# Loading the accumulators of the second half later, behind small VectorE fills, in a one-core kernel of a gated long convolution and a two-layer ReLU network

## The chip, the core and the metric

The kernel runs on one core of a Trainium2 chip. The core has five engines that run side by side and wait for one another through semaphores: TensorE (PE in the profile; PEld is its weight load), VectorE (DVE), ScalarE (ACT), GpSimd (POOL) and SyncE (SP). SP does no arithmetic here; it issues most of the DMA transfers, one after another, in a fixed order. The metric is the device time of one execution in microseconds (us). Before the change the median of three runs is 1064.95 us (1064.24 to 1065.45).

## The reference, cut to what matters

`x` is `A_q`, 2048 rows of 576 columns, in float32. With `xn = layernorm(x)` the output is

```python
k_shift = short causal convolution of k (4 taps per channel)
kv = k_shift * v
y  = long causal convolution of kv with ssm_k per channel   # by FFT, length 2 * 2048
A  = xn * (y + kv * ssm_D)
h  = relu(xn @ w1)               # 576 -> 4608
B  = h @ w2                      # 4608 -> 576
out = x + A + B
```

## The kernel before

**The network.** The 2048 rows are 16 row tiles t of 128 rows (T = 16), in four blocks of four (BT = 4): block 0 is t 0 to 3, block 1 is 4 to 7, block 2 is 8 to 11, block 3 is 12 to 15. The 4608 hidden columns are 18 pairs of 128 (NPAIR = 18). The first half of the program takes blocks 0 and 1 through all pairs, the second half blocks 2 and 3. Its outer loop walks over `visits`, numbered q: each visit is one pair n of hidden columns (n from 18 on in the second half) for one block in place s (0 or 1). A visit of the second half has four stages, st 0 to 3 (`quad`): a Strassen-like set of products into two PSUM banks (tiles `psa` and `psb`, line 542) with a few VectorE additions (lines 597 and 600) between them, then the ReLU, split into a rounded high part `hh` (ACT, line 548) and the remainder `ll` (DVE, line 549). All matrices are split in such high and low parts, so that three float32r products make up one float32 product.

**The sums.** After each stage `fill()` takes up to two units from a queue of work. A unit (line 629) multiplies `hh` and `ll` by `w2` for one row tile and one half of the 576 columns, into one of three PSUM tiles `pso`, and DVE adds it to the accumulator `acc` (line 634 or 638). The accumulators hold x at first: `load_acc(t)` loads the rows of tiles t and t + 1 into one SBUF tile, in two DMAs of 288 KB (helper `load_x`, DMA line 160). There are only eight rows' worth of places, two pair tiles for each of two tags. Blocks 0 and 3 share one tag, blocks 1 and 2 the other. So the place of the pair (12, 13) is free only when the finished sums of the pair (0, 1) have been stored to `fin` (line 646, DMA of 576 KB), 14 follows 2, 8 follows 4 and 10 follows 6. In the names below `acc12` is the pair tile (12, 13), and `fin<-acc0` is the store of the pair (0, 1).

**The convolution.** It runs as a second stream of instructions (`conv()`), of which `tick()` places a piece between the matmuls of the network whenever the network's cost has grown enough. Its part `fm` is just beginning where the change lies: for each group g it loads two tiles of 288 KB, `ztk` and `ztx` (line 886; `ztk2` is that of k in group 2), splits each on ACT into `hik` or `hix` (line 893) and on DVE into `lok` or `lox` (line 894), multiplies by a 128 x 128 matrix into PSUM tiles `psf` (line 904, three places), copies the results for k out on ACT (lines 934 and 935), moves half of each by a DMA inside SBUF (`k<-k`, lines 937 and 938), copies those for x out swapped (`sw`, lines 945 and 946) and multiplies the two on DVE (line 947).

**The weights.** For each coming pair SP loads `both_w1` (lines 440 and 442) and `r2` (line 449); ACT rounds them (lines 466 and 528), POOL makes the low parts (line 428) and, in the second half, the sums of blocks of w1 (line 495).

**What sets the order.** The order on each engine is written into the program before it runs. It comes from a scheduler that places each instruction when a model of the machine says it is ready, in the order of the program; `here()` ties an instruction behind the latest accumulation and the latest ACT instruction of the network, so that it isn't placed early. SP then issues in that fixed order and stops at the first DMA whose semaphores aren't there. SP's DMAs also take eight landing counters in turn (DMAHW0 to DMAHW7 in the listings below), and each waits until the DMA that last used its counter, eight places ahead, has landed.

In the kernel before, all four loads are called behind the last stage of a visit:

```python
        if half == 1 and m == 0:
            base = HT + (1 - second) * BT
            for t in range(base, base + BT, 2):
                load_acc(t)
```

Of the kernel before, what the change touches and what calls it, by code (L numbers as in the profile page):

```python
# [22 lines left out]
T = S // P  # L23
# [5 lines left out]
NPAIR = DFF // FC  # L29
HR = 256  # L30
NB = 4
BT = T // NB
HALVES = 2
HB = NB // HALVES
HT = T // HALVES
# [74 lines left out]
def h3_ffn_kernel(ctx: ExitStack, tc, x, k, v, shift_k, ssm_k, ssm_D, w1, w2, fwd, inv, mid, out):  # L110
    nc = tc.nc
# [37 lines left out]
    def place(b):  # L149

        return 1 - b if b < HB else b - HB

    def halves(u):

        return slice(u * A1, (u + 1) * A1), slice((1 - u) * A1, (2 - u) * A1)

    def move(tile_, rows, t, store=False, queues=(nc.sync, nc.sync)):
        for u in range(U):
            a, b = tile_[halves(u)[0]], rows[u, :, t]
            queues[u].dma_start(*((b, a) if store else (a, b)))  # L160

    pairs = {}

    def load_x(t, tag, bufs, **queues):
        pair = xp.tile([P, 2, D], F32, tag=tag, name=f"acc{t}", bufs=bufs)
        move(pair, x, slice(t, t + 2), **queues)
        return pair

    def load_acc(t, **queues):
        pairs[t] = load_x(t, f"acc{place(t // BT)}", BT // 2, **queues)  # L170
        acc[t], acc[t + 1] = pairs[t][:, 0, :], pairs[t][:, 1, :]

    def stats(t, src):
        st = xp.tile([P, 2, 6], F32, tag="bn", name=f"bn{t}", bufs=4)
        for h in range(2):
            nc.vector.bn_stats(st[:, h, :], src[:, h * NH:(h + 1) * NH])  # L176
        nc.vector.bn_aggr(mv[:, t, :], st)

    def inv_std(t0, n):

        q = xp.tile([P, 3, BT], F32, tag="q", name=f"q{t0}")[:, :, :n]
        va, h0, qu = q[:, 0, :], q[:, 1, :], q[:, 2, :]
        nc.vector.tensor_scalar(va, mv[:, t0:t0 + n, 1], EPS, None, op0=OP.add)
        nc.scalar.activation(h0, va, AF.Sqrt, scale=0.25)
        nc.vector.reciprocal(qu, h0)
        nc.vector.tensor_tensor(qu, va, qu, OP.mult)
        nc.vector.scalar_tensor_tensor(qu, qu, 0.25, h0, op0=OP.mult, op1=OP.add)
        nc.vector.reciprocal(rstd[:, t0:t0 + n], qu)

    def normalized(dst, src, t, cols=slice(0, D)):  # L190
        nc.vector.tensor_scalar(dst[:, cols], src[:, cols], mv[:, t, 0:1], rstd[:, t:t + 1],
                                op0=OP.subtract, op1=OP.mult)
# [21 lines left out]
    def split_low(c, ps, s):  # L214

        if c == 4:
            xr = ops[s, "xr"]
            done["act"] = nc.scalar.activation(xr[:64, :], ps[:64, :], AF.Copy)
            done["dve"] = nc.vector.tensor_tensor(xr[64:, :], ps[:64, :], xr[:64, :],
                                                  OP.subtract)  # L220
            return None
        to = ops[s, "b2" if c % 2 else "b1"][:, :, c // 2]
        last = nc.scalar.activation(to[:, 0], ps, AF.Copy)  # L223
        nc.vector.tensor_tensor(to[:, 1], ps, to[:, 0], OP.subtract)  # L224
        return last

    def row_tiles(s, name):
        t = scratch(s, name)
        return [t[:, i * D:(i + 1) * D] for i in range(BT)]

    def plain_tiles(s):
        for name in ("b1", "b2", "xr"):
            operand(s, name)
# [37 lines left out]
    def turned(c, xn):  # L271
        w = min(P, D - c * P)
        ps = fft_psum()
        for i in range(BT):
            nc.tensor.transpose(ps[:w, i * P:(i + 1) * P], xn[i][:, c * P:c * P + w], ident)
        return ps

    def second_stats(srcs):
        for t in range(BT, BT + 2):
            with tc.issue_after(lows[0].ins):  # L280
                stats(t, srcs[t])

    def second_xT(srcs):

        s = place(1)
        plain_tiles(s)
        with tc.issue_after(done["acc"].ins):
            for t in range(BT + 2, HT):
                stats(t, srcs[t])
            inv_std(BT, BT)  # L290
        xn = row_tiles(s, "xn1")
        for cols in (slice(0, P), slice(P, D)):
            for i, row in enumerate(xn):
                normalized(row, srcs[BT + i], BT + i, cols)
        yield
        for cs in ((0, 1, 2), (3, 4)):
            for c in cs:
                split_low(c, turned(c, xn), s)
            yield
# [146 lines left out]
    def load_w2(n, h):  # L446
        f0 = (n % NPAIR) * FC
        r2 = wp.tile([P, FT, NH], F32, tag="r2", name=f"r2_{n}_{h}", bufs=2)
        nc.sync.dma_start(r2, w2[f0:f0 + FC, h * NH:(h + 1) * NH]
                          .rearrange("(j p) d -> p j d", p=P))  # L450
        raw_w[n, h] = r2
# [72 lines left out]
    def split_w2(n, h):  # L524
        r2 = raw_w[n, h]
        t = wp.tile([P, 2, FT, NH], F32R, tag="w2", name=f"w2_{n}_{h}", bufs=4)
        with at_turn(n):
            nc.scalar.activation(t[:, 0], r2, AF.Copy)  # L528
        last = split_lo(t[:, 1], r2, t[:, 0])
        weights[n]["w2", h] = t  # L530
        return last
# [25 lines left out]
    def mm1(n, s, j):  # L557
        g = weights[n][j]
        ps = bank(j, f"psh{n}_{s}_{j}")
        seq = []  # L560
        for c in range(4):
            b = ops[s, "b2" if c % 2 else "b1"][:, :, c // 2]
            seq += [(g[:, 0, c], b[:, 0]), (g[:, 0, c], b[:, 1]), (g[:, 1, c], b[:, 0])]
        seq += rest(n, j, s)
        for i, (a, m) in enumerate(seq):
            done["pe"] = nc.tensor.matmul(ps, a, m, start=i == 0, stop=i == len(seq) - 1)  # L566
            if i % 7 == 6:
                tick(W_PLAIN / 4)
        relu(n, s, j, ps)
# [88 lines left out]
    def fill():  # L658
        room = 2
        while work and work[0][0] <= room:  # L660
            size, args = work.pop(0)
            unit(*args)
            room -= size
# [23 lines left out]
    @contextmanager  # L687
    def here():


        with tc.issue_after(done["acc"].ins), tc.issue_after(done["act"].ins):
            yield
# [433 lines left out]
    visits = [(0, place(0)), (1, place(0)), (0, place(1)), (1, place(1))]  # L1126
# [36 lines left out]
    def later_w2(n, h):  # L1163
        with tc.issue_after(done["act"].ins):
            split_w2(n, h)
        if n + 1 < HALVES * NPAIR:
            load_w2(n + 1, h)
# [3 lines left out]
               (3, 0): [(split_plain, 2, 0)], (3, 1): [(split_plain, 2, 1)],  # L1171
               (3, 3): [(split_rest, 2), (load_w1, 4)],
               (5, 1): [(later_w2, 2, 0)], (6, 0): [(later_w2, 2, 1)]}
    rest_of_block = second_xT(acc)
    for q, (n, s) in enumerate(visits):
        half, m = divmod(n, NPAIR)
        b = HB + s if half else 1 - s
        second = q % 2
        if q == 2:
            for _ in rest_of_block:  # L1180
                fill()
        parts = quad(n, s, q % 2) if half else None
        for st in range(4):
            if half:
                next(parts)
            elif st % 2 == 0:
                mm1(n, s, st // 2)
                if q < 2:
                    done["acc"] = lows[-1]
            if q == 0 and st == 2:  # L1190
                second_stats(acc)
            for what, *args in opening.get((q, st), ()):
                what(*args)
            if q > 3:
                split_next(n, second, st)
                if st == 1 and n > 2:
                    later_w2(n, second)
            if half:
                tick(W_STAGE[st])
            if q > 3 and (st % 2 or st == 2 and q % 2):  # L1200
                next(ahead, None)
            fill()
        if m == NPAIR - 1 and not half:
            fetch(s, ("b1", "b2", "xr"))
        if n == NPAIR - 2 and not half:
            for _ in ahead:
                pass
            fetch(s, ("t",))
        last = m == NPAIR - 1
        if q in (1, 3):  # L1210
            phase([0, 1], s, b, False)
        elif q > 3 and second == 0:
            phase([n] if m == (0 if half else 2) else [n - 1, n], s, b, last)
        elif last:
            phase([n], s, b, True)
        if half == 1 and m == 0:
            base = HT + (1 - second) * BT
            for t in range(base, base + BT, 2):
                load_acc(t)
    while work:  # L1220
        fill()
    rest_of_stream()
# [27 lines left out]
```

## Time and profile before

| | |
|---|---|
| median of 3 runs | 1064.95 us (1064.24 to 1065.45) |
| the profiled execution's own time | 1063.99 us |
| its span (first to last instruction) | 1062.2 us |
| time of the execution that lies outside the span | 1.8 us |
| mean granted TensorE clock | 0.998 of full speed |
| engine busy shares: PE, DVE, ACT, POOL | 99%, 70%, 52%, 38% |
| moved by DMA | 204.45 MB, mean 192 GB/s |

The profile names instructions by the line of the kernel and by tiles without their numbers: `acc<-in_x` is any load of line 160 into an accumulator. A row of the timeline gives the start and the duration in us, the engine, line, operation, and in brackets how long the engine was idle just before and what ended that. SPq is the queue of DMA issues on SP: the duration of such a row is that of the issue, not of the transfer. Of several merged issues (x2) the duration covers any wait between them.

### The profile page before, as it was taken

The numbers are of one execution on the slowest core, as the hardware profiler recorded it, in microseconds if no ns is written. First come the engines' busy times: TensorE is split into PE (matmuls) and PEld (weight loads), VectorE is DVE, ScalarE is ACT, GpSimd is POOL, SyncE is SP. The second block draws the span as 40 slices with busy tenths as digits, with TensorE's granted clock in tenths as the row PEclk, the third lists the DMA queues.
The fourth block names the chain that finished last, engine by engine and source line by source line (L and its number), as shares of the span: only waits on it lengthen the run. The fifth ranks groups of instructions, "written<-read, shape, count | busy, mean of one in ns | idle before, by whom it ended". The sixth has DMA issues, their size and how long they took to land.

```text
span 1062.2 us, 20038 instructions
## 1 busy us (share of the span) xinstructions
PE 1048.8 (99%) x7153; PEld 989.5 (93%) x7153; DVE 744.0 (70%) x1312; ACT 551.3 (52%) x1201; POOL 398.6 (38%) x398
## 2 busy tenths in 40 slices
PE   8999999999999999999989999999999999999998
PEld 5889999989999999999989999999999999999997
DVE  4539778787777788772458787878777873666664
ACT  4226566534343443433267877687777773443441
POOL 4133333333332233243324434334333444544641
PEclk9999999999999999999999999999999999999999
DMA  9944867687566766856876656666566648776964
GB/s 225 208 97 133 226 173 209 203 229 205 152 192 175 205 193 181 262 144 216 255 197 185 176 171 180 175 192 189 163 178 190 182 126 255 225 224 215 287 193 112
DMA packets 156303, 204.45 MB, mean 192 GB/s; under 512 B 32845, under 2 KB 122703, under 8 KB 155180
## 3 DMA queue, kind: packets, MB, share of 16 engines
q1 hardware_dynamic: 143308, 189.00, 60.8%
q0 software_dynamic: 12576, 13.44, 5.6%
q8 instruction: 56, 0.92, 0.4%
q10 hardware_dynamic: 320, 0.74, 0.3%
q14 instruction: 43, 0.35, 0.1%
HBM read 133.92 MB, written 55.05 MB: 178 GB/s over the span
## 4 chain that ended last, share of the span: by engine, by line
PE 93%; DMA 3%; DVE 2%; ACT 1%; issue 1%; SPq 0%; DVEq 0%; ACTq 0%
PE pso L629 41%; PE psh L566 22%; PE psb L542 12%; PE psf L904 7%; PE psa L542 6%; PE psf L684 3%; DMA acc<-in_x 1%; DMA fin<-acc 1%; PE psf L1048 1%; PE psf L1050 1%; DMA ztk<-zk 1%; DMA zy<-vo 0%; ACT hh L548 0%; DVE bn L176 0%; DVE k L965 0%
## 5 line engine op out<-in xcount | busy, mean ns | idle before, releaser
L629 PE MATMUL pso<-w,hh 128*128 128x288 f32 x2304 | 469.5, 295 | 1.6 <-ACT w L528 0.8
L629 PEld LDWEIGHTS pso<-w,hh 128*128 128x128 f32 x2304 | 373.1, 188 | 9.9 <-ACT w L528 1.2
L629 PE MATMUL pso<-w,ll 128*128 128x288 f32 x1152 | 329.8, 295 | 0.0
L428 POOL TENSOR_TENSOR g<-both_w,g 128x256 fp32r<-128x256 f32 (+2 forms) x145 | 168.2, 1167 | 373.6 <-ACT g L466 320.3
L566 PE MATMUL psh<-b,g 128*128 128x512 f32 x864 | 218.2, 395 | 0.5 <-ACT b L223 0.2
L629 PEld LDWEIGHTS pso<-w,ll 128*128 128x128 f32 x1152 | 213.5, 188 | 1.1
L566 PEld LDWEIGHTS psh<-b,g 128*128 128x128 f32 x864 | 156.9, 188 | 30.5 <-DVE b L224 0.5
L638 DVE TENSOR_TENSOR acc<-pso,acc 128x288 f32<-128x288 f32 x232 | 101.8, 450 | 60.3 <-PE pso L629 59.1
L428 POOL TENSOR_TENSOR w<-r,w 128x576 fp32r<-128x576 f32 x72 | 113.4, 1576 | 56.1 <-ACT w L528 56.0
L548 ACT ACTIVATE hh<-psh 128x512 fp32r<-128x512 f32 x72 | 43.0, 598 | 144.2 <-PE psh L566 144.2
L549 DVE SCALAR_TENSOR_TENSOR ll<-psh,hh 128x512 fp32r<-128x512 f32 x72 | 49.4, 687 | 69.8 <-ACT hh L548 69.4
L542 PE MATMUL psb<-t,g 128*128 128x256 f32 x648 | 94.9, 280 | 0.1
L542 PEld LDWEIGHTS psb<-t,g 128*128 128x128 f32 x648 | 85.5, 188 | 0.4 <-DVE psa L597 0.3
L466 ACT ACTIVATE g<-both_w 128x256 fp32r<-128x256 f32 (+2 forms) x145 | 76.3, 543 | 9.5 <-PE psb L542 6.4
L495 POOL TENSOR_TENSOR both_w<-both_w 128x256 f32<-128x256 f32 x72 | 62.6, 890 | 33.7 <-DMA both_w<-in_w 32.4
L542 PE MATMUL psa<-b,g 128*128 128x256 f32 x432 | 63.1, 280 | 0.0
L548 ACT ACTIVATE hh<-psa 128x512 fp32r<-128x512 f32 x36 | 21.5, 597 | 72.3 <-PE psa L542 72.1
L542 PE MATMUL psb<-b,g 128*128 128x256 f32 x432 | 57.5, 281 | 0.0
L542 PEld LDWEIGHTS psa<-b,g 128*128 128x128 f32 x432 | 56.6, 188 | 0.0
L542 PEld LDWEIGHTS psb<-b,g 128*128 128x128 f32 x432 | 54.4, 188 | 0.2
L947 DVE TENSOR_TENSOR k<-psf,k 128x288 f32<-128x288 f32 x64 | 28.9, 453 | 35.5 <-ACT sw L946 34.2
L670 POOL DMA_DIRECT2D wx<-in_fwd x32 | 17.7, 552 | 95.4 <-PE psf L684 86.7
(134 smaller groups left out, 1697.6 us busy)
## 6 DMA issues: line engine op xcount, KB each, us to landing
r<-in_w SPq DMA_DIRECT2D x72, 288.0 KB, 4.4
zy<-vo SPq DMA_DIRECT2D x64, 288.0 KB, 3.1
zo<-zy SPq DMA_DIRECT2D x32, 576.0 KB, 4.5
both_w<-in_w SPq DMA_DIRECT2D x35, 512.0 KB, 4.2
zk<-zk SPq DMA_DIRECT2D x64, 144.0 KB, 2.5
ztk<-zk SPq DMA_DIRECT2D x32, 288.0 KB, 3.0
ztx<-zx SPq DMA_DIRECT2D x32, 288.0 KB, 3.6
k<-k SPq DMA_DIRECT2D x64, 144.0 KB, 3.4
```

The lines of the kernel that those rows point to most:

```text
L428: return nc.gpsimd.tensor_tensor(dst, src, hi, OP.subtract)
L466: nc.scalar.activation(hi, src, AF.Copy)
L495: nc.gpsimd.tensor_tensor(dst, a, b, op)
L542: done["pe"] = nc.tensor.matmul(ps, a, m, start=start and i == 0, stop=i == len(seq) - 1, skip_group_check=not start)
L548: done["act"] = nc.scalar.activation(hh, ps, AF.Relu)
L549: lows.append(nc.vector.scalar_tensor_tensor(ll, ps, 0.0, hh, op0=OP.max, op1=OP.subtract))
L566: done["pe"] = nc.tensor.matmul(ps, a, m, start=i == 0, stop=i == len(seq) - 1)
L629: done["pe"] = nc.tensor.matmul(ps[:, :NH], a, m, start=c == 0, stop=c == len(seq) - 1)
L638: done["acc"] = nc.vector.tensor_tensor(acc[t][:, dc], ps[:, :NH], acc[t][:, dc], OP.add)
L684: nc.tensor.matmul(ps[:, :NH], w[:, n, :], stk, start=n == 0, stop=n == 1)
L904: nc.tensor.matmul(ps[:, :NH], a, m[:, cols], start=n == 0, stop=n == 2)
L947: nc.vector.tensor_tensor(k1[:, cols], ps, k1[:, cols], OP.mult)
```

## The change

`load_x` may first write a zero into one column of each of the two rows of the pair (a DVE MEMSET of 128 x 2 elements), held by `here()`, and the two DMAs then wait for that fill. The four loads are called from a table, ahead of the units of the named stage: the pair 12 in stage 1 and the pair 14 in stage 2 of visit first_q + 1 (pair n = 18, place 0), the pair 8 in stage 2 and the pair 10 in stage 3 of visit first_q + 2 (n = 19, place 0). The call behind the last stage is gone. first_q is the visit of n = 18 in place 1.

```diff
-    def load_x(t, tag, bufs, **queues):
+    def load_x(t, tag, bufs, late=False, **queues):
         pair = xp.tile([P, 2, D], F32, tag=tag, name=f"acc{t}", bufs=bufs)
+        if late:
+            with here():
+                nc.vector.memset(pair[:, :, :1], 0.0)
         move(pair, x, slice(t, t + 2), **queues)
         return pair
...
+    first_q = visits.index((NPAIR, place(T // BT - 1)))
+    acc_loads = {(first_q + 1, 1): [T - BT], (first_q + 1, 2): [T - BT + 2],
+                 (first_q + 2, 2): [HT], (first_q + 2, 3): [HT + 2]}
...
                 if st == 1 and n > 2:
                     later_w2(n, second)
+            for t in acc_loads.get((q, st), ()):
+                load_acc(t, late=True)
             if half:
                 tick(W_STAGE[st])
...
-        if half == 1 and m == 0:
-            base = HT + (1 - second) * BT
-            for t in range(base, base + BT, 2):
-                load_acc(t)
```

In the listings below a row is the line, the operation and its tiles; lines of the changed kernel are higher by 3 from `load_x` on (line 886 is 889, 638 is 641). The first two listings are SP's queue from the store of the pair (2, 3) on. In the brackets stand the landing counters and engines that a DMA waits for. Before:

```order
L646 DMA fin_89<-acc2_100 128x1152 [waits DMAHW1_49,DVE_49]
L160 DMA acc14_5825<-in_x 64x1152 [waits DMAHW1_49]
L160 DMA acc14_5825<-in_x 64x1152
L646 DMA fin_89<-acc4_229 128x1152 [waits DMAHW4_49,DVE_49]
L886 DMA ztx1_5970<-zx_85 128x576 [waits DMAHW5_49,DVE_49]
L449 DMA r2_19_1_5883<-in_w2 128x2x288 [waits DMAHW6_49,Pool_49]
L160 DMA acc8_6019<-in_x 64x1152 [waits DMAHW7_49,DMAHW4_49]
L646 DMA fin_89<-acc6_232 128x1152 [waits DMAHW0_49,DVE_49]
L160 DMA acc8_6019<-in_x 64x1152
L160 DMA acc10_6022<-in_x 64x1152 [waits DMAHW2_49,DMAHW0_49]
L160 DMA acc10_6022<-in_x 64x1152 [waits DMAHW3_49]
L886 DMA ztk2_6007<-zk_86 128x576 [waits DVE_49]
```

The same stretch of SP's queue after the change:

```order
L649 DMA fin_89<-acc2_100 128x1152 [waits DMAHW7_49,DVE_49]
L160 DMA acc12_5879<-in_x 64x1152 [waits DMAHW2_49,DVE_49]
L160 DMA acc12_5879<-in_x 64x1152 [waits DMAHW1_49]
L160 DMA acc14_5927<-in_x 64x1152 [waits DMAHW7_49,DVE_49]
L160 DMA acc14_5927<-in_x 64x1152
L649 DMA fin_89<-acc4_229 128x1152 [waits DMAHW4_49,DVE_49]
L889 DMA ztx1_5972<-zx_85 128x576 [waits DMAHW5_49,DVE_49]
L452 DMA r2_19_1_5877<-in_w2 128x2x288 [waits DMAHW6_49,Pool_49]
L649 DMA fin_89<-acc6_232 128x1152 [waits DVE_49]
L889 DMA ztk2_6009<-zk_86 128x576 [waits DMAHW0_49,DVE_49]
L443 DMA both_w1_94<-in_w1 128x4x256 [waits DMAHW1_49,Pool_49]
L445 DMA both_w1_94<-in_w1 64x256 [waits DMAHW2_49,Pool_49]
```

The loads of 12 moved behind the store of (2, 3) (before they stood ahead of it); those of 14 stay behind that store, which they wait for through the counter DMAHW7; those of 8 and 10 no longer stand between the store of (6, 7) and `ztk2`. They now stand ten places further on, behind the load of `r2` of pair 20:

```order
L940 DMA k1_1_6011<-k1_1_6011 64x576 [waits Activation_49]
L941 DMA k2_1_6012<-k2_1_6012 64x576 [waits DMAHW1_49,Activation_49]
L452 DMA r2_20_0_6094<-in_w2 128x2x288 [waits DMAHW2_49,Pool_49]
L160 DMA acc8_6146<-in_x 64x1152 [waits DMAHW3_49]
L160 DMA acc8_6146<-in_x 64x1152 [waits DMAHW4_49]
L160 DMA acc10_6200<-in_x 64x1152 [waits DMAHW5_49]
L160 DMA acc10_6200<-in_x 64x1152 [waits DMAHW6_49]
L889 DMA ztk4_6216<-zk_86 128x576 [waits DMAHW7_49,DVE_49]
```

Their DVE wait is gone from these rows because an earlier DMA of the queue already waits for a later DVE instruction than the fills.

On DVE the first two fills stand between the accumulations of block 1 (`pso17_4_0` is pair 17, row tile 4, column half 0). After the change:

```order
L641 TENSOR_TENSOR acc4_229<-pso17_5_0_5850,acc4_229 128x288
L168 MEMSET acc12_5879 128x2
L552 SCALAR_TENSOR_TENSOR ll18_1_1_5803<-psb18_1_5678,hh18_1_1_5802 128x512
L641 TENSOR_TENSOR acc6_232<-pso17_6_0_5889,acc6_232 128x288
L641 TENSOR_TENSOR acc6_232<-pso17_7_0_5897,acc6_232 128x288
L168 MEMSET acc14_5927 128x2
L641 TENSOR_TENSOR acc4_229<-pso17_4_1_5935,acc4_229 128x288
L641 TENSOR_TENSOR acc4_229<-pso17_5_1_5943,acc4_229 128x288
L897 TENSOR_TENSOR lok0_5884<-ztk0_5776,hik0_5883 128x576
L600 TENSOR_TENSOR psa18_0_5823<-psb18_0_5822,m5_18_0_5836 128x256
```

Without the two MEMSET rows this is the order before. The fill of 12 waits for the landing of the store of (0, 1), the fill of 14 for that of (2, 3). The fills of 8 and 10 stand later on DVE, the first behind the addition of `pso18_15_0`, the second behind that of `pso18_13_1` and ahead of `lok2`.

The order of PE is the same in both kernels. On ACT two instructions change places, `w2_19_0` (line 528) and `hik2` (line 893). Before, and then after the change:

```order
L593 ACTIVATE psa19_0_6026<-psb19_0_6025 128x256
L528 ACTIVATE w2_19_0_6095<-r2_19_0_5727 128x576
L893 ACTIVATE hik2_6074<-ztk2_6007 128x576
L934 ACTIVATE k1_1_6009<-psf_6011 64x288
```

```order
L596 ACTIVATE psa19_0_6022<-psb19_0_6021 128x256
L896 ACTIVATE hik2_6070<-ztk2_6009 128x576
L531 ACTIVATE w2_19_0_6091<-r2_19_0_5727 128x576
L937 ACTIVATE k1_1_6011<-psf_6013 64x288
```

`hik2` now stands directly behind the copy into `psa`. On POOL two of the four sums of line 495 for pair 20 move ahead of the low part of `w2_19_0`.

## The prediction

> **What bounds the kernel now.** I read the busy shares first, then what PE waited for, then the chain of waits around the one long wait, and there the timelines of PE, ACT, SP and DVE. The shares, from the page, and PE's longest waits (us in total, times, longest):
>
> ```profile
> PE 1048.8 (99%) x7153; PEld 989.5 (93%) x7153; DVE 744.0 (70%) x1312; ACT 551.3 (52%) x1201; POOL 398.6 (38%) x398
> ...
> PE psf L904 <- ACT k L935: 4.0, 1, 4.0
> PE psw L1109 <- DVE table L1103: 1.2, 1, 1.2
> ...
> PE pso L629 <- ACT w L528: 0.8, 1, 0.8
> ```
>
> PE is the bound. All its waits but the first row belong to the start of the program. So time can be won in the middle only at that one place, a wait of 4.0 us of a convolution matmul for ACT. The chain of waits through it (start, length, what):
>
> ```profile
> 516.47 7.96 DMA fin<-acc
> ...
> 531.21 4.66 DMA fin<-acc
> ...
> 537.06 5.35 DMA ztk<-zk
> ...
> 543.48 0.41 ACT k L935
> ...
> 543.94 1.09 PE psf L904 x3
> ```
>
> Read backwards: PE waits for a PSUM place that ACT empties at line 935; ACT stood at `hik2`, which waits for the load `ztk2`; that load was issued only at 537.06. The timelines say why (PE, then ACT, then SP, and from the waits of SP the row for line 160):
>
> ```profile
> 539.62 0.30 PE L629 MATMUL pso<-w,ll 128*128 128x288 f32 x1
> 543.94 0.61 PE L904 MATMUL psf<-hix,m_sb 128*128 128x288 f32 x1 [4.02 <-ACT k L935]
> ...
> 535.81 0.67 ACT L528 ACTIVATE w<-r 128x576 fp32r<-128x576 f32 x1
> 542.49 0.68 ACT L893 ACTIVATE hik<-ztk 128x576 fp32r<-128x576 f32 x1 [6.01 <-DMA ztk<-zk]
> ...
> 516.47 0.37 SPq L646 DMA_DIRECT2D fin<-acc  x1
> ...
> 531.21 0.54 SPq L646 DMA_DIRECT2D fin<-acc  x1
> 531.79 5.21 SPq L160 DMA_DIRECT2D acc<-in_x  x3
> 537.06 0.58 SPq L886 DMA_DIRECT2D ztk<-zk  x1
> ...
> SPq L160 <- DMA fin<-acc: 16.0, 4, 7.6
> ```
>
> SP stands four times, 16.0 us together, at loads of x whose place a store still holds. The last time, behind 531.79, it stands at the loads of 10 until the store of (6, 7) has landed, near 535.9, and `ztk2` is behind them. This is the head-of-queue wait that the change takes away.
>
> The stall costs more than its 4 us:
>
> ```profile
> 500.56 3.19 PE pso L629 x24
> ...
> 20.00:22.60 2.60, 1.81 (x10) 1.24 (x9) 1.92 (x7) 2.05 (x4) 0.94 (x2) 1.00 1.11 321
> ...
> 543.94:546.96 3.02, 3.02 (x12) 3.02 (x13) 1.87 (x5) 2.92 (x7) 1.78 (x2) 0.51 1.04 246
> ```
>
> Elsewhere such a matmul follows the last after 3.19 / 24 = 0.133 us. Behind the stall (windows; the number behind the brackets is the granted clock) 12 matmuls took 3.02 us at a clock of 0.51. The short stall of 0.8 us at 21 us, inside the first window, left the clock at 1.00.
>
> **The change, part by part.**
>
> *Gone: the stall.* The matmul of 543.94 was due 0.133 us behind 539.62, at 539.75: 4.19 us. The slow clock: 3.02 - 12 x 0.133 = 1.42 us. Together 5.61 us, if nothing else stops PE there.
>
> The Trainium skill, page "TensorE: Matmul & The Clock Gate", section "Part 1: The HAM clock gate", says that an idle stretch of about 3.4 us halves the array's clock and that about as long a busy one restores it. The trace agrees: 4.02 us idle, then 0.51 for 3.02 us. By that rule a leftover stall under 3.4 us would lose no clock, so a stall half removed would still give back the 1.42 us.
>
> *Is `ztk2` early enough?* Without the loads ahead of it SP reaches it behind the store of (6, 7). Then it waits for its buffer, which `lox0` on DVE frees, and its landing counter for the loads of 12, issued over 10 us before. The DVE row, and two windows for the rate of the DMAs (the last number is GB/s):
>
> ```profile
> 530.40 1.13 DVE L894 TENSOR_TENSOR lox<-ztx,hix 128x576 fp32r<-128x576 f32 x1
> ...
> 513.50:524.50 11.00, 11.00 (x86) 10.82 (x86) 5.82 (x11) 3.81 (x8) 3.24 (x3) 1.00 0.77 213
> 524.50:535.90 11.40, 11.40 (x89) 11.23 (x88) 7.81 (x15) 6.03 (x15) 4.01 (x4) 1.00 0.82 259
> ```
>
> So `ztk2` goes out near 531.6 rather than 537.06. With the 5.35 us that it took before, it lands at 537.0. That is the late end, since the 1.18 MB of the loads of 8 and 10 no longer go out beside it. At 259 GB/s half of that is 2.3 us, which gives 534.7 as the early end. ACT comes to `hik2` at 535.8 either way (the row of `w2_19_0`, whose place it takes). I take 535.8.
>
> *The work that hides it from there.* What follows on ACT and DVE was packed tightly behind `hik2` in the trace. Its last two DVE rows, and the PE product behind them:
>
> ```profile
> 545.48 1.04 DVE L894 TENSOR_TENSOR lox<-ztx,hix 128x576 fp32r<-128x576 f32 x1 [1.15 <-ACT hix L893]
> 546.45 0.44 DVE L947 TENSOR_TENSOR k<-psf,k 128x288 f32<-128x288 f32 x1
> ...
> 548.16 0.87 PE L542 MATMUL psb<-t,g 128*128 128x256 f32 x6
> ```
>
> From the start of `hik2` to the end of the multiplication of line 947 it took 546.89 - 542.49 = 4.40 us. Now `w2_19_0` (0.67) lies in between: 535.8 + 4.40 + 0.67 = 540.9. PE needs that multiplication 18 matmuls after the old stall, at 539.75 + 18 x 0.133 = 542.1, for a PSUM place; the product of 548.16, which also needs the line 597 addition queued behind it on DVE, 21 matmuls after, at 542.5. So 1.2 us are to spare, and `ztk2` may land at 537.0 without stopping PE: the cost is nothing, covered by these 18 matmuls; each us beyond 537.0 costs one.
>
> *What is late next: the copies `k<-k`.* The multiplication also needs the copies of group 0, which stand behind the loads of `both_w1`, and those wait for POOL's low parts of g. The POOL row, SP's rows, and from the page the size and median landing time of such a copy:
>
> ```profile
> 532.83 1.44 POOL L428 TENSOR_TENSOR g<-both_w,g 128x256 fp32r<-128x256 f32 x2 [1.92 <-ACT g L466]
> ...
> 537.73 0.39 SPq L440 DMA_DIRECT2D both_w<-in_w  x1
> 538.22 1.11 SPq L442 DMA_DIRECT2D both_w<-in_w  x2
> 539.38 0.59 SPq L937 DMA_DIRECT2D k<-k  x1
> 540.07 0.54 SPq L938 DMA_DIRECT2D k<-k  x1
> ...
> k<-k SPq DMA_DIRECT2D x64, 144.0 KB, 3.4
> ...
> 545.18 4.04 POOL L495 TENSOR_TENSOR both_w<-both_w 128x256 f32<-128x256 f32 x4 [7.19 <-DMA both_w<-in_w]
> ```
>
> POOL is done at 534.3; SP then needs the same 2.34 us up to the second copy, 536.6. With 3.4 us it lands at 540.0, in time for 540.5, when by the same sum `lox1` (ended 546.52) leaves DVE. The other end is the crowded queue: `both_w1`, issued from 537.73, had landed only at 545.18. The last of its three issues began near 538.8, so took some 6.4 us; a copy so slow lands at 543.0, and the multiplication would end at 543.5, 1.4 us behind 542.1. Range 0 to 1.4 us; the row of the copies is the nearer, I take 0.3.
>
> *Added: four fills on DVE.* The kernel has such fills of one to three columns:
>
> ```profile
> L739 DVE MEMSET both<- x3: 61/61/61, 27.0 to 44.1; 128x3 f32 x3
> ...
> 521.19 0.46 DVE L638 TENSOR_TENSOR acc<-pso,acc 128x288 f32<-128x288 f32 x1 [1.31 <-PE pso L629]
> 523.54 1.49 DVE L894 TENSOR_TENSOR lok<-ztk,hik 128x576 fp32r<-128x576 f32 x1 [0.30 <-DMA fin<-acc]
> ...
> 526.38 0.86 PE L542 MATMUL psb<-t,g 128*128 128x256 f32 x6
> ```
>
> Four times 0.06 us on an engine that is 70% busy: nothing. Their waits are what matters, since DVE stands still meanwhile. The fill of 12 waits for the store of (0, 1). The first of SP's four waits was for that store, and it was over before SP issued the next one at 516.47, which the fill stands behind: no wait. The fill of 14 comes behind the addition of 521.19, at 521.7, and waits for the store of (2, 3), which landed at 516.47 + 7.96 = 524.4. Queued behind it are two additions (0.46 each), `lok0` (1.49) and the addition of line 597 (about 0.4 by its 256 columns), which the product of 526.38 waits for. If the store lands at T, that product can start at T + 2.8. At T = 524.4 PE loses 0.8 us. But the two halves of 12's load, 0.59 MB, no longer lie ahead of that store: at 213 GB/s 2.8 us less, T = 521.6, and then the cost is 0. Range 0 to 0.8, I take 0.3, since that load now goes out right behind the store and may share some of its time.
>
> The Trainium skill, page "DMA: Bandwidth & Descriptors", section "Queues, rings and completion order", says that each DMA engine takes the descriptors of one queue in the order of issue. By it the loads of 12, now issued behind that store, could not delay it, and this term would be 0. The trace alone can't show it.
>
> The fills of 8 and 10 wait for the stores of (4, 5) and (6, 7). In DVE's order they stand behind `lox0`, which ends at 531.5. The first of these stores had landed before SP issued the second at 531.21; the fill of 10 stands right ahead of `lok2`, which needs `hik2` (535.8 + 0.67) anyway, and its store had landed by 531.21 + 4.66 = 535.9. Neither goes out later than before, since SP no longer stands at the loads of 8: nothing.
>
> *Moved: the eight loads.* The number of issues and bytes stays. The load of 14 goes out at T, no later than before. The loads of 8 and 10 go out behind `r2` of pair 20, which waits for POOL's `w2_19_0`, and that for two sums of line 495 behind the landing of `both_w1`. Issued at 534.3 to 535.9 and taking 6.4 us, it lands by 542.3; two sums (half of 4.04) and 1.4 us for the low part: 545.8; five issues and a landing of 4.5 us: near 552.5.
>
> ```profile
> acc<-in_x SPq DMA_DIRECT2D x8, 288.0 KB, 4.5
> ...
> 557.88 0.81 DVE L638 TENSOR_TENSOR acc<-pso,acc 128x288 f32<-128x288 f32 x2
> ```
>
> The first addition into 8 was at 557.88, 5.6 us earlier is 552.3. Even this late end is within 0.2 us, and two more PSUM places lie between it and PE: nothing.
>
> *Sum.* 5.61 - 0.3 - 0.3 = 5.0 us. The profiled execution's own 1063.99 becomes 1059.0. It lay 0.96 below the median of 1064.95; from that, **1059.9 us**. The bounds of the terms alone: 5.61 won (1059.3) to 5.61 - 1.4 - 0.8 = 3.4 (1061.5).
>
> **The rivals.**
>
> *A new stall in the same place.* `ztk2` or the copies land 2 to 4 us later than I take them, because the stores, `both_w1` and loads still go through one crowded queue. For it: 6.4 us for `both_w1`. Against: 1.18 MB less in that stretch. PE then stops 2 to 3 us near 542; the clock may or may not fall. Time 1062 to 1063.
>
> *No change.* `ztk2` lands at 541 or later, or the stall comes back as a whole at `both_w1` or the loads of 8 and 10. For it: every step behind hangs on the same few DMAs. Against: it would need over 9 us from issue to landing, against 5.35. Time 1064 to 1066.
>
> *Slower: DVE held at the fill of 14.* Where before only SP waited for the store of (2, 3), now DVE does, and all additions queue behind it. PE's stall is T + 2.8 - 526.4, and the clock's 1.42 comes on top when it is long. Without this term 5.3 us are won; the stall eats them up from T near 527.5, and time is lost beyond what can be measured from T near 529.6, 13 us behind the issue of 516.47. At T = 530.5 the time is 1064.95 - 5.3 + 6.9 + 1.4 = 1068. Against: the store took 7.96 us, with more ahead of it.
>
> **How the numbers follow.** Forecast 0.68, a new stall 0.18, no change 0.08, slower 0.06. A measurement of this kernel tells about 0.2%, 2.1 us, from no change, so faster means under 1062.8. The forecast and most of the second case lie there: 0.84 faster, 0.10 the same, 0.06 slower. The range: from the full 5.61 less the 0.6 us by which runs differ, 1058.7, up to the middle of the second case, 1062.4.
>
> **What would show it.** PE's wait of 4.0 us for line 935 gone, and its clock 1.00 between 540 and 550; SP's waits for stores, 16.0 us, down to those that DVE's fills take over; `ztk2` issued near 531.6. DVE idle before the fill of 14, under 2.8 us; a PE wait for the line 597 addition there of under 1 us. The forecast is wrong if PE shows a wait of over 2 us anywhere between 505 and 560, or if `hik2` starts behind 538.

## The result, and the profile after

The changed kernel takes **1058.1 us** (median of 6 runs, 1057.84 to 1058.26), the kernel before 1064.62 us in the 6 runs beside it (1063.33 to 1065.45). The ratio is 0.9932, 95% interval 0.992 to 0.9944: about 0.7% faster. Forecast were 1059.9 us and a range of 1058.7 to 1062.4; the time lies 0.6 us under that range.

First the head of the changed kernel's page and PE's longest waits (us in total, times, longest):

```profile
span 1056.2 us, 20042 instructions
...
PE 1047.1 (99%) x7153; PEld 988.2 (94%) x7153; DVE 743.9 (70%) x1316; ACT 550.7 (52%) x1201; POOL 398.2 (38%) x398
...
PE psw L1112 <- DVE table L1106: 1.2, 1, 1.2
PE pso L632 <- ACT w L531: 0.8, 1, 0.8
PE psf L262 <- DVE xn L200: 0.8, 1, 0.8
```

The wait of 4.0 us for line 935 (938 now) is gone, and no other stands in its place; what is left belongs to the start. Next SP's queue in the stretch of the change, from the timeline, and from SP's waits the row for the loads of x:

```profile
515.50 0.32 SPq L649 DMA_DIRECT2D fin<-acc  x1
517.06 6.90 SPq L160 DMA_DIRECT2D acc<-in_x  x4
524.05 0.54 SPq L649 DMA_DIRECT2D fin<-acc  x1
...
526.12 1.07 SPq L649 DMA_DIRECT2D fin<-acc  x1
531.10 0.32 SPq L889 DMA_DIRECT2D ztk<-zk  x1
...
540.06 3.19 SPq L160 DMA_DIRECT2D acc<-in_x  x4
...
SPq L160 <- DMA fin<-acc: 4.1, 1, 4.1
```

SP's waits for stores fell from 16.0 us to 4.1: behind 517.06 it still stands ahead of the loads of 14, for the store of (2, 3). `ztk2` went out at 531.10 rather than 537.06, and the loads of 8 and 10 behind 540. This execution runs 0.47 us ahead of the earlier one when it comes to this stretch (539.15 below against 539.62 for the same matmul), so 531.10 is 531.57 in the clock of the prediction. ACT and DVE in the same stretch, from their timelines:

```profile
535.33 0.67 ACT L896 ACTIVATE hik<-ztk 128x576 fp32r<-128x576 f32 x1
535.90 0.68 ACT L531 ACTIVATE w<-r 128x576 fp32r<-128x576 f32 x1
...
516.96 0.06 DVE L168 MEMSET acc<- 128x2 f32 x1
...
522.61 0.46 DVE L641 TENSOR_TENSOR acc<-pso,acc 128x288 f32<-128x288 f32 x1 [1.43 <-DMA fin<-acc]
522.61 0.06 DVE L168 MEMSET acc<- 128x2 f32 x1
...
524.48 0.42 DVE L600 TENSOR_TENSOR psa<-psb,m 128x256 f32<-128x256 f32 x1
...
540.13 0.44 DVE L950 TENSOR_TENSOR k<-psf,k 128x288 f32<-128x288 f32 x1
```

`hik2` starts as soon as ACT is free; it waits for nothing. DVE stands 1.43 us before the fill of 14, for the store of (2, 3). PE, where the stall was, and its windows (5 us each: busy time of the engines, granted clock, DMA share, GB/s):

```profile
539.15 0.30 PE L632 MATMUL pso<-w,ll 128*128 128x288 f32 x1
539.28 0.30 PE L907 MATMUL psf<-hix,m_sb 128*128 128x288 f32 x1
...
542.07 0.87 PE L545 MATMUL psb<-t,g 128*128 128x256 f32 x6
...
535.00:540.00 5.00, 5.00 (x41) 5.00 (x41) 2.95 (x6) 4.60 (x12) 3.23 (x4) 1.00 0.93 304
540.00:545.00 5.00, 5.00 (x40) 4.91 (x40) 4.39 (x10) 2.24 (x5) 1.55 (x2) 1.00 0.88 232
```

The matmul that had to wait follows the last after 0.13 us, and the clock stays at 1.00.

### The profile page after: what moved, and what is told of

Same layout as the page of the kernel before. It is cut to its first block, busy times and chain, and to the rows that moved or that the text cites. A ratio compares the mean times of both kernels' runs of the same rounds, so it can differ in the third digit from the quotient of the medians.

```text
span 1056.2 us, 20042 instructions
## 1 busy us (share of the span) xinstructions
PE 1047.1 (99%) x7153; PEld 988.2 (94%) x7153; DVE 743.9 (70%) x1316; ACT 550.7 (52%) x1201; POOL 398.2 (38%) x398
## 4 chain that ended last, share of the span: by engine, by line
PE 97%; DVE 1%; DMA 1%; ACT 0%; issue 0%; SPq 0%; DVEq 0%
PE pso L632 43%; PE psh L569 22%; PE psb L545 14%; PE psf L907 7%; PE psa L545 6%; PE psf L687 3%; PE psf L1051 1%; PE psf L1053 1%; DMA acc<-in_x 1%; DVE bn L179 0%; PE psf L278 0%; ACT hh L551 0%; DVE lok L897 0%; DVE acc L641 0%; DVE yl L932 0%
```

## The experiments

The question left was not whether the stall went, but why 1.8 us more came out than forecast. **Theory S**: the stall itself differs from execution to execution, and the profiled one was a short case. **Theory B**: the executions differ by an offset that the change leaves alone. Beside them stood **A** (only the place of the loads of 8 and 10 ahead of `ztk2` mattered) against **R** (the loads of 12 and 14 did), and **C** (a hold of DVE costs only what outlasts the slack behind it).

### The kernel before, once more

No edit.

> The kernel before, profiled once more and timed in five more executions. Theory S (the stall itself varies: its length hangs on DMA landings and on where the slow clock begins and ends): the profile shows again one PE wait for line 935 near 540 with a slow clock behind it, but of another size than 4.0 us and 1.4 us, and what lies ahead of 505 us and behind 560 us takes the same time as in the first profile within 0.3 us; the runs spread over 1.5 us or more (1063.3 to 1065.5 so far), where the changed kernel spread over 0.4 us. Theory B (the runs differ by a common offset, at the start of the program or outside the span): the wait is 4.0 us within 0.2 and the difference of times lies ahead of 60 us or outside the span.

Measured: 1065.13 us, median of 12 runs, from 1063.95 to 1067.03; the 23 other runs of the kernel before in that series lie between 1062.93 and 1067.37. The stalled matmul with the one before it, the window behind it, and SP at the loads of 8 and 10, all from this second profiled execution (span 1064.8 us, time 1066.59):

```profile
539.59 0.30 PE L629 MATMUL pso<-w,ll 128*128 128x288 f32 x1
545.53 0.61 PE L904 MATMUL psf<-hix,m_sb 128*128 128x288 f32 x1 [5.64 <-ACT k L935]
...
545.53:550.74 5.21, 5.21 (x22) 5.21 (x22) 2.90 (x8) 2.99 (x7) 2.84 (x4) 0.50 0.94 228
...
533.97 5.27 SPq L160 DMA_DIRECT2D acc<-in_x  x3
539.28 0.58 SPq L886 DMA_DIRECT2D ztk<-zk  x1
```

The same stall in the same place, but 545.53 - 539.72 = 5.81 us long instead of 4.19, and behind it 21 matmuls took 5.21 us at half the clock, 5.21 - 21 x 0.133 = 2.42 us more than at full. Together 8.2 us instead of 5.61. The span differs by 2.6 us between the two executions, the stall and its slow clock by the same 2.6. The matmul ahead of the stall stands at 539.59 and stood at 539.62. From the product of line 542 behind the stall (548.16 and 550.74) to the end of the span it is 514.0 and 514.1 us. So for these two executions theory S holds and B falls: what differs is the stall.

### The loads called later, but without fills

```diff
-                load_acc(t, late=True)
+                load_acc(t)
```

> The four loads are called at the new places but without the fills. The scheduler then puts them into SP's queue exactly where they were before. Theory A (what counts is the place in SP's queue, and only the fills hold the loads back there): the stall is as before, time 1063.3 to 1065.5. Rival (calling them later is enough, as other names of buffers or other landing counters free the queue): time under 1061.

Measured: 1065.31 us (1062.95 to 1068.09), ratio 1.0, interval 0.999 to 1.001. SP's order there is that of the kernel before, and so is the stall (SP at the loads of 8 and 10, the stalled matmul with the one before it, and the window behind it):

```profile
532.60 5.16 SPq L160 DMA_DIRECT2D acc<-in_x  x3
537.81 0.58 SPq L889 DMA_DIRECT2D ztk<-zk  x1
...
539.58 0.30 PE L632 MATMUL pso<-w,ll 128*128 128x288 f32 x1
544.38 0.61 PE L907 MATMUL psf<-hix,m_sb 128*128 128x288 f32 x1 [4.50 <-ACT k L938]
...
544.38:549.55 5.17, 5.17 (x22) 5.17 (x22) 3.98 (x9) 2.98 (x7) 3.76 (x4) 0.51 1.04 254
```

Calling the loads later does nothing alone; the scheduler, which follows its model of when a place is free, puts them back. The fills are what moves them in SP's queue. This execution is a third sample of the stall: 4.50 us of wait, then 21 matmuls in 5.17 us, so 4.67 + 2.38 = 7.05 us in all; its span of 1063.5 less 7.0 is 1056.5. The other two are 1064.8 - 8.2 = 1056.6 and 1062.2 - 5.6 = 1056.6. The changed kernel has 1056.2, without a stall.

### Only the loads of 8 and 10 late

```diff
-    acc_loads = {(first_q + 1, 1): [T - BT], (first_q + 1, 2): [T - BT + 2],
-                 (first_q + 2, 2): [HT], (first_q + 2, 3): [HT + 2]}
+    acc_loads = {(first_q + 2, 2): [HT], (first_q + 2, 3): [HT + 2]}
...
+        if half == 1 and m == 0 and not second:
+            base = HT + (1 - second) * BT
+            for t in range(base, base + BT, 2):
+                load_acc(t)
```

> Only the loads of 8 and 10 go out late behind fills; those of 12 and 14 are called where they were, without fills. SP's order from the store of (4, 5) on is that of the changed kernel. Theory A (only the loads between the store of (6, 7) and ztk2 mattered): the PE wait for line 935 is gone or under 0.5 us, the time is that of the changed kernel, 1058.1 within 0.5. Rival R (the early loads of 12 and 14 and SP's 7.6 us wait for the store of (2, 3) delay the stores behind it enough): ztk2 is issued over 2 us later than in the changed kernel, a wait of 1 us or more stays, time 1060 to 1062.

Measured: 1058.21 us (1058.08 to 1059.22), ratio 0.9936, interval 0.9923 to 0.9949: the time of the changed kernel. SP's queue, the last matmul ahead of the old stall, and PE's only waits between 60 and 1050 us:

```profile
529.58 1.26 SPq L649 DMA_DIRECT2D fin<-acc  x1
532.20 0.32 SPq L889 DMA_DIRECT2D ztk<-zk  x1
...
539.66 0.30 PE L632 MATMUL pso<-w,ll 128*128 128x288 f32 x1
...
546.47 0.62 PE L545 MATMUL psb<-xr,g 128*128 128x512 f32 x2
...
PE psb L545 <- DVE psb L603: 0.2, 1, 0.2
PE psb L545 <- DVE psa L600: 0.2, 1, 0.2
```

Moving these two loads alone is enough, as theory A says. With SP still held for the store of (2, 3) as before, `ztk2` goes out 1.1 us later than in the changed kernel, 0.6 us counted from that matmul (539.66 against 539.15). Nearly all of that fits into the slack: there are two waits of 0.2 us, and PE loses 0.5 us up to the product of 546.47 (6.81 us behind 539.66, in the changed kernel 6.28). The profiled execution, with 1059.22 us, is the slowest of the six; the others lie between 1058.08 and 1058.26.

### Only the loads of 12 and 14 late

```diff
-    acc_loads = {(first_q + 1, 1): [T - BT], (first_q + 1, 2): [T - BT + 2],
-                 (first_q + 2, 2): [HT], (first_q + 2, 3): [HT + 2]}
+    acc_loads = {(first_q + 1, 1): [T - BT], (first_q + 1, 2): [T - BT + 2]}
...
+        if half == 1 and m == 0 and second:
+            base = HT + (1 - second) * BT
+            for t in range(base, base + BT, 2):
+                load_acc(t)
```

> Only the loads of 12 and 14 go out late behind fills; those of 8 and 10 are called where they were and stand between the store of (6, 7) and ztk2. Theory A: SP issues the store of (6, 7) near 527.5 instead of 531.2, since no load of 8 stands ahead of it, sees it land near 532.3, issues four loads (2.2 us), and ztk2 goes out near 534.5 and lands near 539.5: PE waits about 2.5 us for line 935. If so short a wait leaves the clock alone the time is near 1060.6, if it halves the clock for 3 us near 1062. Rival R (the loads of 12 and 14 were what mattered): no wait, 1058.1.

Measured: 1059.82 us (1058.57 to 1060.32), ratio 0.9949, interval 0.9936 to 0.9962, so 1.7 us over the changed kernel, but 5.6 under the kernel before (1065.39, median of 23 runs beside it). SP, then ACT, then PE and its window behind the wait:

```profile
526.40 0.60 SPq L649 DMA_DIRECT2D fin<-acc  x1
529.38 4.39 SPq L160 DMA_DIRECT2D acc<-in_x  x4
533.82 0.58 SPq L889 DMA_DIRECT2D ztk<-zk  x1
...
539.13 0.68 ACT L896 ACTIVATE hik<-ztk 128x576 fp32r<-128x576 f32 x1 [3.10 <-DMA ztk<-zk]
...
539.17 0.30 PE L632 MATMUL pso<-w,ll 128*128 128x288 f32 x1
540.58 0.40 PE L907 MATMUL psf<-hix,m_sb 128*128 128x288 f32 x1 [1.12 <-ACT k L938]
...
543.86 0.87 PE L545 MATMUL psb<-t,g 128*128 128x256 f32 x6
...
540.58:543.86 3.28, 3.28 (x21) 2.96 (x22) 2.12 (x6) 2.99 (x7) 2.41 (x3) 1.00 0.99 265
```

The store of (6, 7) goes out at 526.40 instead of 531.21, 4.4 us earlier when the 0.45 us are counted by which this execution runs ahead (539.17), but the loads of 8 and 10 still stand between it and `ztk2`, and `hik2` starts 3.8 us later than in the changed kernel. PE loses 540.58 - 539.30 = 1.28 us at the first matmul and, up to the product of 543.86, 21 matmuls behind 539.30, 4.56 - 2.79 = 1.77 us in all. This tests the prediction's slack: it let `ztk2` land up to 537.0, which is 536.55 here, and `w2_19_0` stands ahead of `hik2` here, which gives 0.67 more, 537.2. So 539.13 should cost 1.9 us; it cost 1.77. The 2.5 us that I expected had missed that 0.67, and the time lies 0.8 us under the 1060.6 expected. After 1.12 us of idling the clock stayed at 1.00.

So theory R falls, since a stall is left, but the "only" of theory A is too strong. Moving 8 and 10 alone wins 7.2 us (1065.39 - 1058.21), moving 12 and 14 alone 5.6, and both together end at 1058.1, as the first does. The loads of 8 and 10 ahead of `ztk2` make the stall. How long it is hangs also on when the store of (6, 7) goes out, and that is earlier here, where no load of 8 stands ahead of it in SP's queue.

### DVE held longer

The load of 14 called one stage earlier, which puts its fill one addition earlier on DVE:

```diff
-    acc_loads = {(first_q + 1, 1): [T - BT], (first_q + 1, 2): [T - BT + 2],
+    acc_loads = {(first_q + 1, 1): [T - BT, T - BT + 2],
```

> As the changed kernel, but the load of 14 is called one stage earlier; the scheduler then puts its fill one DVE instruction earlier, ahead of the addition of pso17_7_0 instead of behind it, so DVE comes to it near 519.4 instead of 521.2 and stands still until the store of (2, 3) has landed, near 522.6 in the changed kernel's profile. Theory C (a hold of DVE costs only what outlasts the slack behind it): DVE idle 3.2 us ahead of that fill, twice the 1.4 us of the changed kernel; the additions behind it end 0.45 us later, and PE, whose product of 526.07 is due 1.2 us after the last of them, waits for nothing: 1058.1 within 0.5. Rival (each us that DVE stands still is lost): 1059.9.

Measured: 1058.73 us (1058.15 to 1059.27, 4 runs). DVE, and the one wait of PE in the middle of the program:

```profile
519.45 0.45 DVE L641 TENSOR_TENSOR acc<-pso,acc 128x288 f32<-128x288 f32 x1
524.36 0.46 DVE L641 TENSOR_TENSOR acc<-pso,acc 128x288 f32<-128x288 f32 x1 [4.46 <-DMA fin<-acc]
...
523.30 0.86 PE L545 MATMUL psb<-t,g 128*128 128x256 f32 x6
524.88 0.54 PE L632 MATMUL pso<-w,hh 128*128 128x288 f32 x2 [0.72 <-DVE acc L641]
...
527.37 0.86 PE L545 MATMUL psb<-t,g 128*128 128x256 f32 x6
```

DVE stood still for 4.46 us, 3 us more than in the changed kernel. PE waited 0.72 us and lost 1.0: from the product of 523.30 to that of 527.37 it took 4.07 us, in the changed kernel 3.09 (522.81 to 525.90). So neither the rival (each us of DVE lost) nor the cost of nothing that I expected is right. The store landed later in this execution than I had expected, at 524.36, which is 523.9 in the changed kernel's clock, instead of 522.6; why is open. What outlasted the slack of the PSUM places was lost.

With the finished sums of (2, 3) stored once more, or twice more, to a place that nobody reads, ahead of the load of 12:

```diff
+    aside = dram.tile([1, P, 2, D], F32, name="aside")
...
                     nc.sync.dma_start(fin[t // 2], pairs[t - 1])
+                    if t == 3:
+                        for i_ in range(1):
+                            nc.sync.dma_start(aside[i_], pairs[t - 1])
```

> As the changed kernel, with the finished sums of (2, 3) stored a second time, to a place that nobody reads (0.59 MB more), ahead of the load of 12; the fill of 14 must wait for both stores. The order of DVE is that of the changed kernel. Theory C: at 213 GB/s the second store lands 2.8 us behind the first, T near 525.3 instead of 522.6 in the changed kernel's clock; from T to the product of line 545 it took 2.4 us there at least, so that product starts near 527.7 instead of 526.07: PE waits 1.6 us in all between 523 and 529, the clock stays at 1.00, the time is 1059.7, and ztk2, which has 1.2 us to spare, adds at most 1 us. Rival (DVE's hold is hidden anyway, as in the changed kernel): 1058.1. Rival (a wait of under 3.4 us also slows the clock): 1061 or more.

> As the run with one more store, with two (1.18 MB more). The scheduler now expects the landing later and puts the fill of 14 three instructions later on DVE, behind lok0 and ahead of the addition of line 600. Theory C: T near 528.1 in the changed kernel's clock, the addition of line 600 ends at T + 0.5, so the product of 526.07 starts near 528.7: PE waits 2.6 us there. The stores of (4, 5) and (6, 7), ztx1 and ztk2 all go out later on the same queue, so a second wait for line 938 near 540 can come on top, up to 2 us. Time 1060.5 to 1063. Rival (hidden): 1058.1. If a single wait of 2.6 us halves the clock for 3 us, 1.4 us more.

Measured: 1058.40 us (1058.05 to 1059.86, 4 runs) with one more store, 1059.36 us (1058.55 to 1060.4, 4 runs) with two. In the profile with one more:

```profile
524.08 0.06 DVE L169 MEMSET acc<- 128x2 f32 x1 [2.34 <-DMA aside<-acc]
```

DVE's instructions run 0.56 us behind those of the changed kernel here, so the fill came 0.9 us later than there, not 2.8. The rate of 213 GB/s was taken from a stretch of the kernel before in which the DMA engines were busy for a share of 0.77; in this profile, from the issue of the first store to the fill (516.06 to 524.08), they moved 319 GB/s at a share of 0.92. DVE was held 2.34 us, and PE waited for nothing there, where I had expected 1.6 us. With two more stores the scheduler moved the fill behind `lok0`, DVE stood 0.46 us before it, and the only wait of PE in that profile between 513 and 560 us is 0.3 us near 542, for the multiplication of line 947. Both forecasts of theory C (1059.7, and 1060.5 to 1063) missed, since the stores landed sooner than I had taken. The four runs with one more store overlap with those of the changed kernel. The four with two all lie above them (1057.84 to 1058.26); the profiled one is the fastest of the four, so what the others lost isn't shown. A hold so long that it would cost what the slower rival named was not reached.

## Why the prediction was wrong, point by point

**The stall and its cause: right.** SP's wait at the loads of 8 and 10 with `ztk2` behind it was the cause, and the whole wait went: 1058.21 us when only these two loads are moved. When they alone stay, a stall is left (1059.82), though a shorter one than before.

**The estimates on the path: right in place, 0.6 us too careful.** In the clock of the prediction, `ztk2` was forecast to go out near 531.6 (531.57), `hik2` to start at 535.8 (535.80), the multiplication of line 947 to end at 540.9 (540.57 + 0.47 = 541.04), with 542.1 as the latest. The two deductions of 0.3 us each, for the copies `k<-k` and for DVE's hold, both came out as 0: the multiplication ended in time, and the store of (2, 3) landed at 523.1, in the middle of 521.6 to 524.4, early enough for all that stands behind the fill. Whether the loads of 12 behind that store delayed it, no run here shows. The hold was there, 1.43 us, and was hidden.

**The step that failed: "It lay 0.96 below the median of 1064.95; from that, 1059.9".** I carried the distance of the profiled execution from the median over to the changed kernel, as if it were an offset. It was a part of the stall, which took 5.6, 7.0 and 8.2 us in three executions, because both the landing of the stores and the length of the slow clock differ. The time of these executions (two of the kernel before, one of the run without fills) less their stall is 1063.99 - 5.61 = 1058.4, 1065.28 - 7.05 = 1058.2 and 1066.59 - 8.23 = 1058.4, each within 0.3 us of the changed kernel's 1058.1. By that the median of 1064.95 holds a stall of some 6.6 us; the term of 5.61 was a short case, and the changed kernel is not slower by the 0.96. The 0.6 us of scatter taken off for the lower end was scatter of the stall too: the changed kernel's runs lie within 0.42 us, its profiled execution 0.17 below their median. That the other runs of the kernel before differ by their stalls as well is likely, but only these three were profiled.

**The start.** The last matmul ahead of the old stall stands at 539.62, 539.59 and 539.58 in the three profiles with the full stall, at 539.17 and 539.66 in the two with one pair of loads moved, and at 539.15 in the changed kernel's. The difference is not the change's: the first products of the program begin at 13.2 to 13.8 us in these profiles, whatever the kernel (13.70 in the first profile of the kernel before, 13.34 in its second, which loses 0.34 us near 135 us; 13.28 in the changed kernel's). The two profiled executions that the forecast is measured by differ by 0.47 us there, in favour of the changed kernel. **The sum** then closes: of the 1.85 us between forecast (1059.95 before rounding) and result, 0.96 - 0.17 = 0.79 is the carried offset, 0.6 the two deductions, 0.47 the start.

**The rivals.** No new stall, no loss. The second case had a stall of 2 to 3 us near 542; late loads of 12 and 14 alone leave one of 1.77 us, from 539.30 on. The moved loads of 8 and 10 cost nothing, as forecast, and went out from 540.06 on instead of near 546.

## What to carry to other kernels

A queue that issues in a fixed order is held by its first waiting transfer: look for what stands behind it, since the load that stopped PE was not the one that waited. Before an estimate is moved from one profiled execution to a median, ask whether the scatter of the runs comes from the very stall that the change removes; here the runs scattered over 2 to 5 us with the stall and over 0.42 without it, and the gain was that of a middling stall, not of the profiled one. Two halves of a change can each win most of what both win together (7.2 and 5.6 us here), so try each alone before saying which was needed. A wait that is moved to an engine with slack behind it costs what outlasts that slack: here 1.4 and 2.3 us of DVE standing still cost PE nothing, 4.5 us cost 1.0.

## What the runs showed that I had not expected

The slow clock behind a PE wait is not of one length: 3.0 us behind 4.02 us of waiting, 5.2 us behind 4.50 and behind 5.64, at a granted clock of 0.50 to 0.51, and none behind 1.12. So of the stall's cost between 1.4 and 2.4 us came from the clock. The slow stretch begins while PE still waits. Windows of the first profile, of the second, and of the run without fills, where the idle stretch ahead of it is shown too:

```profile
543.50:546.91 3.41, 2.97 (x12) 2.98 (x13) 2.26 (x5) 3.29 (x8) 1.73 (x2) 0.50 1.05 244
...
544.09:550.92 6.83, 5.39 (x22) 5.39 (x23) 3.81 (x8) 4.39 (x10) 2.84 (x4) 0.50 0.97 250
...
539.88:542.65 2.77, 0.00 (x0) 0.00 (x0) 0.00 (x0) 0.00 (x0) 0.00 (x0) 1.00 0.96 260
542.65:549.48 6.83, 5.10 (x21) 5.10 (x22) 4.64 (x9) 4.39 (x10) 3.69 (x4) 0.50 1.05 261
```

The clock is halved for 3.41 us in one execution and for twice that, 6.83, in the other two, so one profile of a stall doesn't tell what the clock costs. The Trainium skill, page "TensorE: Matmul & The Clock Gate", section "Part 1: The HAM clock gate", gives about 3.4 us both for losing and for regaining the clock. In the run without fills PE had idled for only 2.77 us when the clock fell, and 6.83 us is twice the figure; here the measurement decides.

And 0.59 MB more in the queue ahead of a wait moved the landing by 0.9 us where the measured rate of that stretch had promised 2.8.
